# Two attention layers on one Trainium2 core: the second linear pass as an ordered pipeline, its end moved into the steps of the first row maxima

## The chip, the cores and the metric

The kernel runs on one core of one Trainium2 chip. The metric is the device time of one execution in microseconds (us); lower is better. The kernel before took 1602.39 us, the median of three runs (1594.55 to 1605.56). All engines of the core work on the same problem: PE multiplies matrices and transposes, DVE, ACT and POOL work on tiles in SBUF, and SP issues the DMAs. Each engine takes its instructions in the order of its own queue and waits at an instruction whose inputs or buffers are not ready. What stands behind a waiting instruction on that engine waits too. The trace's times are those of one profiled execution, counted from the start of its span.

## What is computed

The input x has 2048 rows of 512 numbers, in 32 heads of 16. Four layers add to it in turn, A, B, A, B:

```python
x = x + A(layernorm(x))     # A, per head:
#   pq, pk = q @ w_phi, k @ w_phi
#   phi(p) = [softmax(p), softmax(-p)]             32 features
#   o = phi_q (phi_k^T v) / (phi_q (sum of phi_k)); A = o @ wo
x = x + B(layernorm(x))     # B, per head, four segments of 512 rows, s = 0..3:
#   p = softmax(q k^T / 4 + causal mask) @ v       inside the segment
#   m = phi(q) M / (phi(q) z + 1e-6)               memory of the segments before
#   o = g m + (1 - g) p;  M += phi(k)^T v;  z += sum of phi(k);  B = o @ wo
```

All arithmetic is in float32. A projection is done as three products of a high and a low part (hi x hi, lo x hi, hi x lo), each of which PE takes at its fast rate.

## The kernel before

**Layer A in two passes.** The first pass (`pass1`, L564) goes over the four segments, the last one being segment 0 (`SEGS`). For a segment it normalises and transposes the rows (`norm_T`, L353), projects k, q and v, forms the features of k and adds phi_k^T v to an accumulator, whose end is the tile `KN`. For q it keeps the projected rows: those of segment 0 stay in SBUF as `P` tiles, those of the others go to memory (`pq`) with their row extremes (`mmq`). The second pass (`pass2`, L737) goes over the 16 tiles of 128 rows. For tile i: take the differences of pq and its extremes on POOL, the exponential on ACT, the reciprocals of the sums on DVE and their product on POOL (`feats`, L731, with `differences` L519, `scale_q` L544); transpose the features on PE in two halves, which ACT copies out of PSUM; multiply them by KN on PE; divide on DVE (`weigh`, L448: rows `tmp`); transpose the divided rows of the tile before (`turn`, L419: ACT makes `oh`, DVE makes `ol`); multiply by wo (`out_proj`, L438); and add the residual on DVE, which SP then writes. PSUM tiles of the name `g` come from three banks (`G`).

**Layer B as a table of steps.** `steps` (L1059) runs a counter k from -31 to 163. From k = -9 on a step computes products for row maxima (PE `mx`, DVE `mx` and `mxs`), from k = 0 on also logits and exponentials (PE `lg`, ACT `P`), and PE's product with v follows (`pv`). Everything else (projections of q, k and v, norms, memory, output, the first pass of the next layer A) is put into single steps by the tables `BEFORE`, `FIRST`, `GAPS`, `LAST`, `FINAL`. `opening` (L1048) comes ahead of `steps`: `start` (L785) lets SP fill parts of the four tiles of Q and K with the mask and ones, the first norm of layer B is taken to its 11th step (loads of x, statistics, normalisation), and the weights bwv and the first two slices of wqk are loaded (`queue_w`, L805).

**Who sets the order.** A scheduler orders the instructions of each queue by its own model, except where the program adds dependences: `Ordered` (L153) chains what is issued on DVE, ACT, POOL and SP while `ordered[0]` is set, and `held` (L173) chains PE's while `strict[0]` is set. Before the change, the second pass has neither. The main loop takes 63 yields of it (`A20`, L41), runs the whole opening, sets PE's order as strict, and gives the rest of the pass to `steps`, which spreads it over the slots k = -31 to 1 up to an amount of PE work (`LEFT`, L38). DVE, ACT, POOL and SP are ordered from k = -9 (`ORDERED`, L40). So SP could issue early what stands late in the program: it issued the slices of wqk at 174.68 us and bwv at 180.60, in the first pass, and the loads of the norm as soon as their rows had been written.

**The start.** In the first layer `pass1` loads ident, bd and z, two halves of the raw k weights, x, and the other raw weights. It normalises the first rows while the k weights are folded with w_phi (`folded`, L278), splits the weights (`bring`, L237), and projects v.

Of the kernel before, what the change touches and what calls it, by code (L numbers as in the profile page):

```python
# [7 lines left out]
F32 = mybir.dt.float32  # L8
# [7 lines left out]
D = 512  # L16
H = 32
DH = 16
# [87 lines left out]
def interleave_kernel(ctx, tc, x_in, a_wqkv, a_wphi, a_wo, b_wq, b_wk, b_wv, b_wo, b_beta,  # L106
# [88 lines left out]
    sync.dma_start(out=ident, in_=c_ident)  # L195
    bd = cp.tile([P, 25], F32, name="bd")
    sync.dma_start(out=bd, in_=c_bd)
# [80 lines left out]
    def folded(raw, banks=None):  # L278
# [8 lines left out]
        def get(kc, pf=None):  # L287
            if pf is None:
                pf = PS("g", G)
            for c in range(NC):  # L290
                mm(pf[:, c * P : (c + 1) * P], lhsT=wT[:, c, kc * P : (kc + 1) * P],
                                 rhs=phibd[:, c].rearrange("p h f -> p (h f)"), start=True, stop=True)
            return pf
        if banks is None:
            return get
        done = [get(kc, banks[kc // 2][:, kc % 2]) for kc in range(NC)]
        return lambda kc: done[kc]

    wph = T2("z16", 1, shape=(P, NC, DH))
    sync.dma_start(out=wph, in_=a_wphi.rearrange("(c h) d f -> (h d) c f", c=NC))  # L300
    phibd = sp.tile([P, NC, 8, DH], F32, tag="KN", bufs=1, name="phibd")
    for c in range(NC):
        pool.tensor_tensor(out=phibd[:, c], in0=wph[:, c, :].unsqueeze(1).broadcast_to([P, 8, DH]),
                                in1=bd[:, 16:24].unsqueeze(2).broadcast_to([P, 8, DH]), op=MUL)
# [48 lines left out]
    def norm_T(xsrc, s, hT, spare=False, slow=False, off=False):  # L353

        st = T2("st", 2, shape=(P, 4, 8))
        xt = []
        for t in range(4):
            x = T2("x", 4)
            sync.dma_start(out=x, in_=xsrc[4 * s + t])
            xt.append(x)  # L360
        yield
        for t, x in enumerate(xt):
            bs = T2("bs", 2, shape=(P, 6))
            dve.bn_stats(bs, x)
            dve.bn_aggr(st[:, t, 0:2], bs)
            if t < 3:
                yield
        var, r, u = st[:, :, 1], st[:, :, 2], st[:, :, 3]
        dve.tensor_scalar(var, var, 1e-5, None, op0=ADD)
        yield  # L370
        act.activation(u, var, AF.Ln)
        act.activation(r, u, AF.Exp, scale=-0.5)
        if slow:
            yield
        eng = pool if off else dve
# [5 lines left out]
        eng.tensor_scalar(u, u, -1.0, None, op0=MUL)  # L381
        if slow:
            yield
        for t in range(4):
            act.activation(xt[t], xt[t], AF.Identity, bias=st[:, t, 3:4], scale=st[:, t, 2:3])
# [3 lines left out]
        if spare:  # L389
            hh, hl = wtiles("e8")  # L390
        else:
            hh = hp_.tile([P, NC, D], F32R, tag="hh", bufs=1, name=nm("hh"))
            hl = hp_.tile([P, NC, D], F32R, tag="hl", bufs=1, name=nm("hl"))
        hT[:] = [hh, hl]
        for t in range(4):
            pt = PS("g", G)
            for kc in range(NC):
                tp(pt[:, kc * P : (kc + 1) * P], xt[t][:, kc * P : (kc + 1) * P], ident)
            pv = pt.rearrange("p (k t) -> p k t", k=NC)
            c0 = t * P  # L400
            hv = hh[:, :, c0 : c0 + P]
            act.copy(hv, pv)
# [825 lines left out]
```

## Time and profile before

| what | value |
|---|---|
| median of 3 runs | 1602.39 us (1594.55 to 1605.56) |
| profiled execution | 1599.14 us |
| its span, first to last instruction | 1597.4 us |
| mean granted clock of PE | 0.989 |
| busy share PE, DVE, ACT, POOL | 95%, 71%, 49%, 40% |
| first product with KN, layers 0 and 2 | 204.30 and 983.23 us |
| first product for maxima (k = -9), layer 1 | 316.66 us |
| first logits (k = 0), layer 1 | 348.05 us |
| first projection of v, layer 0 | 19.46 us |

A row of a timeline or of a group has the start, the time, the engine, the line, the operation, the tile written and the tiles read (without their numbers), shapes and the count; in brackets the idle time of the engine ahead of it, and what ended it. `PEld` is the load of weights into PE, which lies beside its products. A row of the waits names the engine that waited, what released it, the sum, the number of waits and the longest. A row of the windows gives the stretch and the busy time of each engine in it, then the granted clock as a share of full speed, the share of DMA time and GB/s. In the chain, each piece is what the next piece was waiting for. In the layers numbered from 0, A is 0 and 2, and B is 1 and 3; "the first pair" is layers 0 and 1.

### The profile page before, as it was taken

How to read it: one execution, taken by the hardware profiler on the slowest of the kernel's cores; microseconds unless marked ns; L12 is line 12 of the kernel's file. 1: busy time of each engine (PE TensorE's matmuls, PEld its weight loads, DVE VectorE, ACT ScalarE, POOL GpSimd, SP SyncE). 2: the span in 40 equal slices, each digit the busy share in tenths (PEclk: the TensorE clock that was granted, in tenths of full speed). 3: DMA queues.
4: the chain of work that ended last, by engine and by line, in shares of the span. 5: the costliest groups of instructions: out<-in, count | busy, mean ns of one | idle time of the engine just before them, and what ended most of it. 6: DMA issues, size and time to landing. Idle time of an engine off the chain costs nothing.

```text
span 1597.4 us, 28178 instructions
## 1 busy us (share of the span) xinstructions
PE 1512.8 (95%) x9856; PEld 1080.8 (68%) x9856; DVE 1127.4 (71%) x3286; ACT 789.6 (49%) x1180; POOL 638.9 (40%) x970
## 2 busy tenths in 40 slices
PE   7999999988999999999989999999889999999997
PEld 6888877855566666665568888877556666666554
DVE  5665776477788887878555648656787788787783
ACT  6544335335665565555433323443465655655543
POOL 1566643313444454333231337431234444443322
PEclk9999999999999999999999999999999999999999
DMA  8446543234433533534322125342353443433330
GB/s 319 132 142 221 204 137 122 100 103 150 127 106 100 153 94 100 153 94 138 103 105 77 36 95 168 122 145 87 111 171 97 109 137 101 107 115 99 81 105 36
DMA packets 101124, 195.76 MB, mean 123 GB/s; under 512 B 13560, under 2 KB 27128, under 8 KB 97912
## 3 DMA queue, kind: packets, MB, share of 16 engines
q1 hardware_dynamic: 99832, 193.44, 39.2%
q8 instruction: 79, 1.29, 0.3%
q10 hardware_dynamic: 1152, 0.52, 0.1%
q14 instruction: 61, 0.50, 0.1%
HBM read 101.05 MB, written 39.85 MB: 88 GB/s over the span
## 4 chain that ended last, share of the span: by engine, by line
PE 67%; DVE 16%; DMA 5%; ACT 4%; issue 4%; POOL 3%; SPq 1%; DVEq 0%; POOLq 0%; ACTq 0%
PE g L185 39%; DVE mx L163 9%; PE mx L185 9%; PE lg L185 8%; PE pv L185 7%; PE g L189 5%; POOL P L163 3%; DVE mxs L163 2%; DMA x<-x 1%; ACT P L163 1%; ACT tb L163 1%; DVE es L163 1%; SPq L163 1%; DVE bs L163 1%; DVE ta L163 1%
## 5 line engine op out<-in xcount | busy, mean ns | idle before, releaser
L163 DVE CUSTOM_DVE_ANT_0 mx<-mx,mask 128x128 f32<-128x128 f32 (+3 forms) x1024 | 510.9, 499 | 172.4 <-PE mx L185 137.4
L163 ACT ACTIVATE P<-lg 128x1024 f32<-128x1024 f32 x320 | 328.7, 1027 | 181.3 <-PE lg L185 172.3
L163 POOL TENSOR_SCALAR_AFFINE_SELECT P<-P 128x256 f32<-128x256 f32 (+1 forms) x448 | 190.1, 439 | 469.2 <-ACT P L163 467.9
L185 PE MATMUL mx<-e,e 63*128 63x256 f32 (+2 forms) x1024 | 155.7, 360 | 29.7 <-DVE mxs L163 21.9
L185 PE MATMUL g<-hh,wqk 128*128 128x512 f32 x512 | 180.7, 407 | 0.7 <-ACT mt L163 0.7
L185 PE MATMUL g<-w,oh 128*128 128x512 f32 x512 | 173.4, 421 | 4.0 <-ACT oh L163 2.7
L185 PE MATMUL lg<-e,e 64*128 64x256 f32 (+2 forms) x1024 | 168.3, 386 | 7.7 <-ACT P L163 5.6
L185 PE MATMUL g<-w,hh 128*128 128x512 f32 x512 | 168.3, 408 | 2.5 <-ACT tb L163 1.4
L185 PE MATMUL pv<-P,v 128*32 128x512 f32 (+3 forms) x2048 | 166.3, 441 | 0.0
L185 PEld LDWEIGHTS lg<-e,e 64*128 64x128 f32 x1024 | 81.1, 184 | 102.8 <-issue 54.2
L163 DVE DVE_READ_ACCUMULATOR2_ANT mxs<- 128x1 f32 x1024 | 144.7, 141 | 0.0
L185 PEld LDWEIGHTS mx<-e,e 63*128 63x128 f32 x1024 | 83.0, 185 | 80.0 <-DVE mxs L163 55.4
L185 PEld LDWEIGHTS pv<-P,v 128*32 128x32 f32 x2048 | 53.8, 109 | 99.2 <-issue 88.7
L163 POOL TENSOR_SCALAR tb<-tb 128x512 f32<-128x512 f32 x48 | 71.4, 1488 | 102.5 <-ACT tb L163 102.5
L185 PEld LDWEIGHTS g<-w,oh 128*128 128x128 f32 x512 | 91.8, 195 | 28.6 <-issue 6.0
L185 PEld LDWEIGHTS g<-hh,wqk 128*128 128x128 f32 x512 | 96.3, 188 | 21.8 <-ACT mt L163 1.2
L185 PEld LDWEIGHTS g<-w,hh 128*128 128x128 f32 x512 | 91.9, 190 | 24.0 <-ACT tb L163 3.5
L163 ACT CAST ta<-g 128x512 fp32r<-128x512 f32 x64 | 37.5, 586 | 135.7 <-PE g L185 135.7
L185 PE MATMUL g<-w,ol 128*128 128x512 f32 x256 | 102.5, 402 | 1.1 <-DVE ol L163 1.1
L185 PE MATMUL g<-w,hl 128*128 128x512 f32 x256 | 101.4, 396 | 0.0
L185 PE MATMUL g<-hl,wqk 128*128 128x512 f32 x256 | 100.2, 391 | 0.0
L185 PE MATMUL g<-w,e 128*128 128x512 f32 x384 | 98.2, 397 | 0.8 <-ACT tb L163 0.8
(122 smaller groups left out, 2601.9 us busy)
## 6 DMA issues: line engine op xcount, KB each, us to landing
e<-ta SPq DMA_DIRECT2D x384, 128.0 KB
wqk<-wqk SPq DMA_DIRECT2D x64, 512.0 KB
x<-x SPq DMA_DIRECT2D x48, 256.0 KB
xr<-in SPq DMA_DIRECT2D x28, 256.0 KB
pq<-tb SPq DMA_DIRECT2D x24, 256.0 KB
tb<-pq SPq DMA_DIRECT2D x24, 256.0 KB
x<-xr SPq DMA_DIRECT2D x24, 256.0 KB
xr<-x SPq DMA_DIRECT2D x24, 256.0 KB
```

The source lines that it names most:

```text
L163: i = f(*a, **k)
L185: return held(nc.tensor.matmul(*a, **k))
L189: return held(nc.tensor.transpose(*a))
```

## The change

1. The second pass is written as a pipeline and kept in written order on all engines, PE too. With tile i, POOL takes the differences of tile i+3, ACT the exponential of i+2, DVE and POOL the scaling of i+1, and SP loads pq of i+4. The rows of the first three tiles come over from the first pass as raw differences.
2. The main loop takes 76 yields of it: all of tiles 0 to 8 but the output of tile 8. `opening` yields after each of its 11 steps of the norm. It is advanced at k = 42, 45, ..., 75: the fills and the loads of x come in tile 5, bwv and two slices of wqk behind the output of tile 7. Then come the 16 transposes of the norm and the projections of `BEFORE`. DVE, ACT, POOL and SP are in written order there too.
3. The rest of the pass (output of tile 8, tiles 9 to 15) goes into the slots k = -9 to 1 alone, in place of -31 to 1 (`LEFT` 44000).
4. The start is a function of its own, `first`, in written order: x is loaded ahead of ident, bd, z and the raw weights; the statistics of all four tiles are one chain; two of the four tiles are normalised on DVE; some low parts go to POOL; q is folded behind the first half of v's projection. Layer A's wq lies in the buffers `e8`, and in the second layer A a spare normalised segment in `w8`. `PREP` goes from 12 to 6, and the first segment of the first pass is strict, with the order k0 k1 q0 q1 v0 k2 k3 q2 q3 v1.
5. At the end of layer B the following work is taken in four single steps around the last turn, and PE's strict order holds to the end.

The number of instructions is the same on PE (8096 in the program), DVE (3286) and SP (795). Two normalisations move from ACT (1243 to 1241) to DVE, and two low parts from DVE to POOL (970 to 972). The core of the diff, with the new function `first` in it:

```diff
@@ -34,15 +34,14 @@
 FILL = (1, 3, 4)
 LEAD = 9
 FINAT = 8
-PAUSE = object()
-LEFT = 53000
+PAUSE, DONE = object(), object()
+LEFT = 44000
 BEGIN = -31
-ORDERED = -9
-A20 = 63
-PREP = 12
+MAXIMA = -9
+A20 = 76
+PREP = 6
 EVERY = (2, 2)
 SEGS = (1, 2, 3, 0)
-AHEAD = 2
 TB2 = 4
 
 
...
+        def first(self, hT, vv):
+
+            ordered[0] = strict[0] = True
+            xt = rows_of(self.xsrc, SEGS[0])
+            wph = T2("z16", 1, shape=(P, NC, DH))
+            sync.dma_start(out=ident, in_=c_ident)
+            sync.dma_start(out=bd, in_=c_bd)
+            sync.dma_start(out=wph, in_=a_wphi.rearrange("(c h) d f -> (h d) c f", c=NC))
+            kraw, vraw, qraw = [fetch(a_wqkv[:, i * D : (i + 1) * D]) for i in (1, 2, 0)]
+            st = T2("st", 2, shape=(P, 4, 8))
+            hT[:] = htiles()
+            (vh, vl), (kh, kl), (qh, ql) = wv, wk, wq = [wtiles(tag) for tag in ("w8", "w8", "e8")]
+            for key, w in (("awv", wv), ("awk", wk), ("awq", wq)):
+                kept[key] = [dtile((P, NC, D), nm(key)) for _ in range(2)]
+                owed.extend(zip(kept[key], w))
+
+            def low(eng, w, kc, raw):
+                eng.tensor_tensor(out=w[1][:, kc, :], in0=raw, in1=w[0][:, kc, :].bitcast(F32), op=SUB)
+
+            for t in range(4):
+                moments(st, t, xt[t])
+            guard(st)
+            root(st)
+            refine(st, dve)
+            for c in range(NC):
+                pool.tensor_tensor(out=phibd[:, c], in0=wph[:, c, :].unsqueeze(1).broadcast_to([P, 8, DH]),
+                                        in1=bd[:, 16:24].unsqueeze(2).broadcast_to([P, 8, DH]), op=MUL)
+            kf, qf = [], []
+            kfold, qfold = folded(kraw, kf), folded(qraw, qf)
+            normal(st, 0, xt[0])
+            for t in (1, 3):
+                dve.tensor_scalar(xt[t], xt[t], st[:, t, 2:3], st[:, t, 3:4], op0=MUL, op1=ADD)
+            next(kfold)
+            next(kfold)
+            normal(st, 2, xt[2])
+            columns(hT, 0, xt[0])
+            columns(hT, 1, xt[1])
+            next(kfold)
+            next(kfold)
+            columns(hT, 2, xt[2])
+            columns(hT, 3, xt[3])
+            next(kfold)
+            for kc in range(NC):
+                act.copy(vh[:, kc, :], vraw[kc])
+                low(pool if kc % 2 else dve, wv, kc, vraw[kc])
+            for kc in range(NC):
+                act.copy(kh[:, kc, :], kf[kc])
+                low(dve, wk, kc, kf[kc])
+            vt = v_tile(hT, wv, vv, ("g", G))
+            for t in range(4):
+                for _ in range(4):
+                    next(vt)
+                if t == 1:
+                    for _ in range(4):
+                        next(qfold)
+            next(qfold)
+            for kc in range(NC):
+                act.copy(qh[:, kc, :], qf[kc])
+                low(dve, wq, kc, qf[kc])
+            ordered[0] = strict[0] = False
+            floor.update(ends)
+            return wq, wk, wv
...
@@ -668,11 +711,15 @@
 
                 if n < NSEG - 1:
                     hTs, vv = [], []
-                    side = chain(norm_T(self.xsrc, SEGS[n + 1], hTs, n % 2 == 0), v_tile(hTs, wv, vv, ("g", G)))
+                    spare = ("e8" if first else "w8") if n % 2 == 0 else None
+                    side = chain(norm_T(self.xsrc, SEGS[n + 1], hTs, spare), v_tile(hTs, wv, vv, ("g", G)))
                     steps = "k0 q0 k1 q1 v0 k2 q2 k3 q3 v1"
+                    strict[0] = first and n == 0
+                    if strict[0]:
+                        steps = "k0 k1 q0 q1 v0 k2 k3 q2 q3 v1"
...
@@ -721,31 +759,23 @@
                         dve.tensor_tensor(out=KN, in0=kva.rearrange("p g (h e) -> p g h e", e=VW),
                                           in1=bdA[:, 0:4].unsqueeze(1).unsqueeze(3).broadcast_to([P, 8, 4, VW]),
                                           op=MUL)
-                        floor.update({k.engine: ends[k.engine] for k in (dve, sync)})
-                        ordered[0] = False
-                strict[0] = False
-                scale(5)
-                self.put_off[4 * s + 2] = lambda: scale_q(e.pop(6))
+                self.e = {4 * s + t: e[4 + t] for t in range(3)}
                 yield
 
-        def feats(self, i):
-
-            pq = T2("tb3", 2)
-            sync.dma_start(out=pq, in_=self.pqs[i])
-            return scale_q(diff_exp(pq, self.mmq[i // 8][:, i % 8]))
+        def load_q(self, i):
+            if i < NT:
+                pq = T2("tb3", 2)
+                sync.dma_start(out=pq, in_=self.pqs[i])
+                self.raw[i] = pq, self.mmq[i // 8][:, i % 8]
 
         def pass2(self):
 
+
             KN = self.KN
             o = None
             for i in range(NT + 1):
                 if i < NT:
-                    j = i + AHEAD
-                    if j in self.put_off:
-                        self.e[j] = self.put_off.pop(j)()
-                    elif j < NT and j not in self.e:
-                        self.e[j] = self.feats(j)
-                    ef = self.e.pop(i)
+                    ef = self.e.pop(i).rearrange("p h s f -> p (h s f)")
                     phT = T2("P4", NP4, shape=(P, 8, P))
                     for half in range(2):
                         pt = PS("g", G)
@@ -753,11 +783,15 @@
                             g = 4 * half + q
                             tp(pt[:, q * P : (q + 1) * P], ef[:, g * P : (g + 1) * P], ident)
                         act.copy(phT[:, 4 * half : 4 * half + 4, :], pt.rearrange("p (g t) -> p g t", g=4))
+                        if half == 1 and i + 1 < NT:
+                            scale_q(self.e[i + 1])
                         yield
                 if i > 0:
                     oT = turn([o[:, c * P : (c + 1) * P] for c in range(NC)])
-                    yield
+                    yield PAUSE if i == NT else None
                 if i < NT:
+                    if i + 2 < NT:
+                        exp(self.e[i + 2])
                     o = T2("tmp", 2)
                     for half in range(2):
                         pn = PS("g", G)
@@ -769,6 +803,9 @@
                         weigh(o[:, half * 256 : half * 256 + 256].rearrange("p (g h d) -> p g h d", g=4, h=4),
                               pv, 0.0, False)
                         yield
+                    if i + 3 < NT:
+                        self.e[i + 3] = differences(*self.raw.pop(i + 3))
+                    self.load_q(i + 4)
                 if i > 0:
                     yield from out_proj(x, self.xdst, i - 1, oT, self.wo)
                 if i < NT:
...
@@ -1052,6 +1091,7 @@
             self.norm0 = self.norm(0)
             for _ in range(11):
                 next(self.norm0)
+                yield
             self.wv = load_w("bwv")
             for _ in range(2):
                 self.queue_w()
@@ -1130,11 +1170,11 @@
                         at_, *what = cell.split()
                         m, j = at_.split(".")
                         table[8 * R * s + R * int(m) + int(j)] = what, s
-            slots = list(range(BEGIN, 2))
+            slots = list(range(MAXIMA, 2))
             spent = 0.0
             for k in range(BEGIN, R * N + 4):
                 m = k // R + 3
-                ordered[0] = ORDERED <= k < R * N
+                ordered[0] = k < R * N
                 if k % R == 0 and 0 <= m < N:
                     self.stack(m)
                 if 0 <= k < R * N:
@@ -1155,22 +1195,29 @@
                     want = LEFT * (1 + slots.index(k)) / len(slots) if k < slots[-1] else 1e9
                     while spent + 100 < want:
                         before = work[0]
-                        if next(side, None) is PAUSE:
-                            break
+                        got = next(side, DONE)
                         spent += work[0] - before
+                        if got is DONE or got is PAUSE and k < slots[-1]:
+                            break
                 what, s = table.get(k, ((), 0))
                 for w in what:
                     do(w, s, k)
                 if k == R * N - 1:
-                    strict[0] = ordered[0] = False
+                    ordered[0] = False
                     floor.update(ends)
             put_off[0] = None
             for f in self.late + self.rows:
                 f()
+            next(after, None)
             self.finish(N - 1)
             for _ in early:
                 pass
-            self.end()
+            for _ in range(2):
+                next(after, None)
+            o = self.end_turn()
+            next(after, None)
+            self.end(o)
+            strict[0] = False
 
     class DTiles:
         def __init__(self, full):
@@ -1190,11 +1237,14 @@
         lb = LayerB(xs[2 * i + 1], xs[2 * i + 2])
         run(p1[i])
         a2 = la[i].pass2()
-        for _ in range(A20):
+        opening = lb.opening()
+        for k in range(A20):
             next(a2)
-        lb.opening()
-        strict[0] = True
-        lb.steps(chain(a2, iter(lambda: PAUSE, 0)), p1[1] if i == 0 else iter(()), FINAL if i else LAST)
+            if k >= 42 and k % 3 == 0:
+                next(opening, None)
+        for _ in opening:
+            pass
+        lb.steps(a2, p1[1] if i == 0 else iter(()), FINAL if i else LAST)
 
 
 def kernel(A_x, A_wqkv, A_w_phi, A_wo, B_x, B_wq, B_wk, B_wv, B_wo, B_beta):
```

More of the change, by code (lines that the diff above doesn't have):

```diff
@@ L276, in plain, with folded @@
         return get
-    def folded(raw, banks=None):
+    def folded(raw, chunks):
         wT = T2("e8", 2 * NSET, shape=(P, NC, D))
@@ L388, in norm_T @@
         yield
[L389 to L394, printed above, removed]
-        for t in range(4):
[L396 to L402, printed above, removed]
-            wait(lambda pv=pv, hv=hv, c0=c0: dve.tensor_tensor(out=hl[:, :, c0 : c0 + P], in0=pv,
-                                                               in1=hv.bitcast(F32), op=SUB))
+        hT[:] = htiles(spare)
+        for t in range(4):
+            columns(hT, t, xt[t])
             yield
@@ L593, in pass1 @@
+                wq, wk, wv = self.first(hTs, vv)
             else:
+                norm = norm_T(self.xsrc, SEGS[0], hTs, slow=True, off=True)
                 for _ in range(11):
@@ L597, in pass1 @@
                 wv = load_w("awv")
-            for _ in norm:
-                yield
-            vt = v_tile(hTs, wv, vv, ("g", G))
-            if first:
-                next(vt)
-                wq = load_w("awq", folded(qraw), "e8")
-            if not first:
+                for _ in norm:
+                    yield
+                vt = v_tile(hTs, wv, vv, ("g", G))
                 for _ in range(8):
```

161 lines of the change are left out of this document (72 added, 89 removed).

## The prediction

> **What bounds the kernel now.** I read the page first, for the engine that fills the span and for the chain that ended last.
>
> ```profile
> span 1597.4 us, 28178 instructions
> PE 1512.8 (95%) x9856; PEld 1080.8 (68%) x9856; DVE 1127.4 (71%) x3286; ACT 789.6 (49%) x1180; POOL 638.9 (40%) x970
> PE 67%; DVE 16%; DMA 5%; ACT 4%; issue 4%; POOL 3%; SPq 1%; DVEq 0%; POOLq 0%; ACTq 0%
> ```
>
> PE is busy for 1512.8 of 1597.4 us, so all its idle time together is 84.6 us. The change gives every engine the same work as before and only moves it. It can therefore win idle time back, or lower-clock time, and nothing else; what it can lose has no such limit. The profiled execution took 1599.14 us, 1.74 above its span and 3.25 below the median of the three runs (1602.39).
>
> Next come the windows over the part that is rewritten, first in the first pair of layers: from the first product with KN to the third step of attention (step 2). The second pair's same part follows. The columns are the window, its length, busy time of PE, PEld, DVE, ACT and POOL, and the granted clock.
>
> ```profile
> 204.30:265.00 60.70, 54.32 (x350) 46.91 (x351) 43.00 (x99) 27.19 (x43) 31.50 (x36) 0.97 0.41 131
> 265.00:316.66 51.66, 50.42 (x291) 42.83 (x290) 23.53 (x51) 20.32 (x34) 16.08 (x20) 1.00 0.35 113
> 316.66:348.05 31.39, 25.55 (x144) 18.06 (x143) 23.14 (x76) 6.92 (x13) 2.75 (x2) 1.00 0.32 101
> 348.05:353.43 5.38, 5.38 (x29) 3.48 (x28) 3.71 (x13) 2.81 (x4) 0.81 (x2) 1.00 0.82 197
> 983.23:1135.17 151.94, 138.74 (x810) 114.20 (x810) 93.69 (x239) 57.25 (x94) 51.18 (x59) 0.97 0.41 129
> ```
>
> The four rows make 149.13 us with PE busy for 135.67: 13.46 idle, 6.38 in the first row and 5.84 in the third, where the first row maxima stand. The clock of 0.97 over 60.70 us is 1.7 us of full-clock time lost, so the stretch holds some 134.0 us of work. The second pair needs 151.94, 2.8 more, all of it in PE's busy time (138.74), that is, in clock. The waits name what the idle time is.
>
> ```profile
> PE g L189 <- DVE ot L163: 2.0, 2, 1.6
> PE g L185 <- ACT P L163: 1.6, 3, 1.1
> PE g L189 <- POOL P L163: 1.5, 1, 1.5
> PE g L189 <- DVE hl L163: 1.0, 1, 1.0
> PE mx L185 <- DVE mxs L163: 2.7, 3, 1.0
> ```
>
> Many short waits, on every engine: there is no single one to take away. (Four rows are from before the maxima, the last from the maxima.)
>
> **The change, part by part.** *The pipeline itself.* PE's rows of one tile of the second pass:
>
> ```profile
> 227.61 1.03 PE L189 MATMUL g<-ident,P 128*128 128x128 f32 x8
> 228.62 0.66 PE L189 MATMUL g<-ident,tmp 128*128 128x128 f32 x4
> 229.11 1.90 PE L185 MATMUL g<-KN,P 128*128 128x68 f32 x16
> 230.82 0.71 PE L185 MATMUL g<-w,oh 128*128 128x512 f32 x2
> 233.66 1.04 PE L189 MATMUL g<-ident,P 128*128 128x128 f32 x8
> ```
>
> One tile is 6.05 us (227.61 to 233.66): 1.01 for the transposes of phi_q, 0.49 for those of the divided product, 1.71 for KN, 2.84 for the output projection. It runs without a gap already. In written order the first pass's last reductions stay ahead of tile 1's on DVE, so the wait on POOL's P (1.5) becomes some 1.8; four following tiles cost about 0.3. Taken: 2.1 idle; bounds 0 to 4.
>
> *The norm's loads on SP.* The opening (mask and ones into the sets, the loads and statistics of layer B's first norm) now starts at k = 42, in tile 5, and SP takes it in written order: the write of x row 3, six fills, then the four loads. SP's rows:
>
> ```profile
> 174.68 1.00 SPq L163 DMA_DIRECT2D wqk<-wqk  x2
> 180.60 0.80 SPq L163 DMA_DIRECT2D w<-bwv  x2
> 202.79 0.70 SPq L163 DMA_DIRECT2D e<-mask  x1
> 204.20 2.50 SPq L163 DMA_DIRECT2D e<-mask  x3
> 208.92 0.63 SPq L163 DMA_DIRECT2D e<-ones  x1
> 211.30 0.56 SPq L163 DMA_DIRECT2D e<-ones  x1
> 217.86 0.39 SPq L163 DMA_DIRECT2D x<-x  x1
> 256.56 2.63 DMA x<-x
> ```
>
> The fills cost SP 0.70 + 2.50 + 0.63 + 0.56 = 4.39 us. They come behind the write that follows the add of tile 3, so with that write and the next residual load (about 1 us) the first norm load is issued some 6 us after the add, and lands 2.63 later (the last row, from the chain): 8.5. On DVE the statistics of that row stand behind tile 5's division, about 3.5 us after the same add by the tile's prices (1.01 + 0.49 + 1.71 and the division's end). Behind them on DVE wait the add of tile 4, which holds its PSUM bank, then the reduction of tile 7, then `ol` of tile 5, for which PE's next projection waits. DVE is 5.0 us late there, a tile has 6.05 us and DVE some 4.8 of work (43.00 in the first window over nine tiles), so about 1.1 is made up and PE loses about 3.9. Bounds 0 (the write is done early) and 5.
>
> *bwv and the first two slices of wqk.* Before, SP issued them at 174.68 and 180.60, with the rest of pass 1 as cover. Now they stand behind the write of x row 7. That write waits for the add of tile 7, which waits for the end of its projection. After that projection PE has only the 16 transposes of the norm. By rows: add 0.69, write 0.6, so the loads start 1.3 us after the projection. A slice of wqk is 512 KB and stands behind 2 MB of bwv: 2.62 MB. The rate and the time to land are in these rows (the first two are the rates in 40 slices of 0.7 us and the hardware queue's sum from 172 to 200 us, with packets, MB and share; the others a load of weights and PE's wait for it):
>
> ```profile
> GB/s 433 398 360 398 407 401 421 378 389 427 345 331 357 401 404 474 354 404 375 410 410 386 222 82 35 0 0 0 0 0 0 0 0 23 0 0 0 0 0 0
> q1 hardware_dynamic: 1983, 6.28, 58.0%
> 826.79 8.87 DMA w<-awq_lo
> 835.71 0.50 PE L185 MATMUL g<-w,hh 128*128 128x512 f32 x1 [1.15 <-DMA w<-awq_lo]
> ```
>
> The transfers fill 23 slices, 16.1 us: 6.28 MB in that time is 390 GB/s, so 2.62 MB take 6.7, and with 1.8 of latency (2.63 less 256 KB at that rate) 8.5: 9.8 after the projection. PE reaches the first q group after 2.0 of transposes and 1.6 of their waits, at 3.6. It waits 6.2 us. Bounds: 3 (wqk overtakes bwv: 0.52 MB need 1.4 + 1.8, and v needs its weights one group later) and 8.9 (the row of awq). Nothing hides it, since PE's order is written out there and nothing else stands before q. The Trainium skill ("DMA: Bandwidth & Descriptors", Specifications) puts a core's limit on its memory at about 358 GB/s; by that the same bytes would take 7.3 and the wait would be an estimated 6.8. The measured 390 lies above the limit, so the trace decides and 6.2 stands.
>
> *16 transposes in a row.* Three PSUM banks for four groups: the fourth waits for ACT's copy and DVE's `hl`. Before, this was the 1.0 on `hl` and part of `ot`; now 1.5 in one place. Bounds 1 and 2.5.
>
> *The maxima.* Tiles 9 to 15 and the end of 8 lie in steps -9 to 1 alone. At step -9 ACT has in front of tile 9's copies what these rows show:
>
> ```profile
> 316.77 0.58 ACT L163 CAST ta<-g 128x512 fp32r<-128x512 f32 x1 [4.62 <-PE g L185]
> 319.91 1.09 ACT L163 ACTIVATE tb<-g 128x512 f32<-128x512 f32 x2 [2.56 <-DVE ta L163]
> 320.88 0.81 ACT L163 ACTIVATE x<-x,st 128x512 f32<-128x512 f32 x1
> 321.58 1.07 ACT L163 COPY P<-g 128x512 f32<-128x512 f32 x2
> ```
>
> The `tb` wait for DVE's `ta`, which is written behind four first maxima. The first copy of a tile ends at 321.58 + 0.53 = 322.11, 5.45 after step -9 began (316.66). PE has 0.49 of maxima, 1.01 of transposes and 0.49 more as cover, 2.0, so 3.5 idle, with handover 3.6. Later steps: PE has about 45.3 us of work there and DVE about 45.8, nearly balanced; taken 2.1 for steps -8 to -1 and 1.9 for steps 0 and 1, where `ol` of tile 15 stands behind maxima. Bounds of the later steps together: 0 and 11.
>
> *Clock.* The rows of the boundary show what idle time costs afterwards:
>
> ```profile
> 815.01 0.66 PE L189 MATMUL g<-ident,U 128*128 128x128 f32 x4 [0.81 <-ACT U L163]
> 819.49 0.66 PE L189 MATMUL g<-ident,tmp 128*128 128x128 f32 x4 [1.75 <-POOL tmp L163]
> 820.82 2.07 PE L185 MATMUL g<-w,oh 128*128 128x512 f32 x4 [0.68 <-ACT oh L163]
> ```
>
> Four matmuls took 2.07 after 1.75 + 0.68 us of idle; two take 0.71 at 230.82. Over the slow stretch that is some 1.7 us. I take two such stretches for each pair, 3.4 us: after the wait of 3.9 or the one of 3.6, and after that of 6.2. The Trainium skill ("TensorE: Matmul & The Clock Gate", What's actually happening) has the clock halve after an idle window of about 3.4 us. By that rule only the 6.2 is sure of it, and the sum would be 1.7 less for each pair. The trace shows a slow stretch after 2.4 us of idle in two pieces, so two are kept.
>
> *The sum for a pair.* 134.0 of work + 2.1 + 3.9 + 1.5 + 6.2 + 3.6 + 2.1 + 1.9 idle + 3.4 clock = 158.7. Against 149.13 that is +9.6, against 151.94 +6.8: together +16.4.
>
> *The start.* Normalisation and folding are rewritten; the first projection of v starts here:
>
> ```profile
> 3.23 1.99 SPq L163 DMA_DIRECT2D x<-in  x4
> 18.70 1.11 PE L189 MATMUL g<-ident,x 128*128 128x128 f32 x4 [1.24 <-DVE hl L163]
> 19.46 1.20 PE L185 MATMUL g<-w,hh 128*128 128x512 f32 x2
> ```
>
> x is now issued first, 2.4 us sooner, but PE's chain also needs ident and the raw weights, which come 2 us later. By my hand count v starts at 18.9 to 19.1: -0.4 us (bounds -3 and +2).
>
> *Boundary and end.* A group of k covers the wait for U (0.81), and wq goes into other buffers, which spares the 1.15 on awq_lo: with the shorter gaps -2.2 (0 to -4.5). Two steps of the following work interleave with the last turn; in the last layer, where nothing follows, the strict order to the end costs 0.3. Earlier preparation and the strict first segment of pass 1 lie beside dense PE work, at nothing (if PE waits there, up to 2).
>
> Sum: 16.4 - 0.4 - 2.2 + 0.3 = +14.1. 1599.1 + 14.1 = 1613.2, taken as 1613.
>
> **Rivals.** *The loads are in time.* If the norm rows are there when DVE wants them and the first slice lands within 3.6 us of the end of tile 7's projection (2.3 after issue), the waits of 3.9 and 6.2 go, and one slow stretch with them: 158.7 - 11.8 = 146.9, that is -2.2 and -5.0, and with the rest 1599.1 - 7.2 - 2.3 = 1589.6. For it speaks that 256 KB alone land in 2.63; against it, that 2 MB go first on the same queue. The point where the change breaks even is a loss of 7.05 less for each pair: both waits together 3.1 instead of 10.1.
>
> *One of the two is hidden.* Only the weights late: 1613 - 7.8 = 1605; only the norm rows late, with a slow stretch less: 1613 - 15.8 = 1597.
>
> *DVE bounds the maxima.* Balanced sums do not mean that the chain copy, KN, division, turn, `ol` fits between maxima: the idle share in the third row is 5.84 of 31.39, 19%. If the eleven steps with 45.3 us of work keep that share, idle time there is 10.6 instead of 7.6, +6 over both; if every one of seven tiles loses 1 us more besides, +20: 1619 to 1633, taken 1626. It decides when DVE ends each step behind PE by more than a PSUM bank covers.
>
> **How the numbers follow.** Late loads in both places, as summed: 0.50, 1604 to 1622. In time: 0.22, 1579 to 1596 (down to where no slow stretch is left either, 3.4 less). One hidden: 0.14. DVE in the maxima: 0.14. The range for 8 in 10, 1588 to 1628, reaches into both rivals and leaves out the lower third of the one and the upper third of the other, with the tails. About 1% is what a measurement of this kernel can tell from no change (its own runs spread over 0.7%); from 1602.39 that puts the bounds at 1586 and 1618. Slower: the DVE case and two fifths of the first, 0.34. Faster: the lower half of the loads in time with its tail, 0.11. Within: 0.55. My likeliest case is within 1%, on the slow side.
>
> **What would show it.** Right: PE idle for 5 to 8 us in front of the first matmul of `g<-hh,wqk` in each pair, released by the DMA of wqk or bwv, with half-speed rows behind it; DVE's first statistics of the norm released by the DMA of x some 4 us late, in tile 5; ACT's copies of P at step -9 behind `tb`. Wrong: q follows the transposes at once; the tiles take 6.1 us through tile 5; the maxima take much more or less than 51 us for steps -9 to -1. A forecast too high by 10 or more means that the loads were not late, and one too low by 10 that DVE sets the pace in the maxima.

## The result, and the profile after

The changed kernel takes 1653.03 us, the median of 6 runs (1650.82 to 1656.99), against 1603.12 for the kernel before in 6 runs. The ratio is 1.0319 with a 95% interval of 1.0287 to 1.0351: 3.2% slower. The forecast was 1613, with a range to 1628. The page of the profile after, its first lines, and PE's own waits (engine, line, what it waited for, the sum, how many, the longest):

```profile
span 1655.3 us, 28153 instructions
PE 1532.1 (93%) x9856; PEld 1094.4 (66%) x9856; DVE 1135.8 (69%) x3286; ACT 786.9 (48%) x1178; POOL 643.3 (39%) x972
```

```profile
PE g L184 <- DVE xr L162: 18.5, 2, 9.7
PE g L184 <- DMA wqk<-wqk: 15.9, 2, 8.1
PE mx L184 <- DVE mxs L162: 15.6, 31, 1.5
...
PE g L188 <- ACT x L162: 8.1, 1, 8.1
PE g L184 <- DVE ol L162: 6.8, 6, 1.7
...
PE mx L184 <- DVE r L162: 4.4, 8, 0.8
```

The span is 57.9 longer. Some 8 of that is the choice of executions: the one profiled before lies 4 under its median (1603.12), the one after 4 over. PE's idle time went from 84.6 to 123.2 (+38.6), and its busy time, for the same products, from 1512.8 to 1532.1 (+19.3). Two waits stand out that were not there before, or only in pieces of up to 1.2: on `xr` and on wqk, twice each, once in each pair. (`xr` and `ot` are tiles with the residual; DVE's add into them frees the PSUM bank that PE writes next. `hh` and `hl` are the high and low parts of the normalised, transposed rows.) By stage:

| from, to | before | after | difference |
|---|---|---|---|
| start to first projection of v | 19.46 | 19.13 | -0.3 |
| to the first product with KN, layer 0 | 184.84 | 193.08 | +8.2 |
| to step 3's logits, layer 1 | 150.80 | 176.24 | +25.4 |
| to the first product with KN, layer 2 | 628.13 | 629.76 | +1.6 |
| to step 3's logits, layer 3 | 153.61 | 175.60 | +22.0 |
| to the end | 460.56 | 461.49 | +0.9 |

So the loss lies in the two rewritten stretches and in the first 60 us. The windows of the first pair after (length, busy PE, PEld, DVE, ACT, POOL, then the granted clock):

```profile
212.21:259.87 47.66, 36.81 (x237) 32.48 (x237) 25.57 (x57) 16.80 (x26) 18.59 (x18) 0.90 0.37 110
259.87:290.80 30.93, 21.38 (x116) 17.93 (x117) 17.42 (x38) 10.54 (x18) 10.85 (x17) 0.78 0.56 196
290.80:314.50 23.70, 23.70 (x97) 19.22 (x98) 5.75 (x12) 6.46 (x13) 4.04 (x8) 0.92 0.58 174
314.50:388.45 73.95, 65.70 (x367) 51.20 (x366) 49.90 (x139) 24.44 (x40) 18.06 (x18) 0.91 0.36 106
```

They add up to 176.24 us with PE busy for 147.58: 28.66 idle. The same stretch before had 136.46 busy and 14.34 idle. The clock is under 1.00 in all four rows; before it was under 1.00 in the first alone. The rows of the timeline behind these windows, PE first, then SP and DVE:

```profile
259.87 1.98 PE L184 MATMUL g<-KN,P 128*128 128x68 f32 x8 [8.79 <-DVE xr L162]
263.00 1.22 PE L184 MATMUL g<-w,oh 128*128 128x512 f32 x2 [1.16 <-DVE ol L162]
290.80 0.77 PE L184 MATMUL g<-hh,wqk 128*128 128x512 f32 x1 [8.06 <-DMA wqk<-wqk]
318.88 1.11 PE L188 MATMUL g<-ident,tmp 128*128 128x128 f32 x4 [2.80 <-ACT tb L162]
320.06 3.68 PE L184 MATMUL g<-KN,P 128*128 128x68 f32 x16
```

```profile
242.92 0.32 SPq L162 DMA_DIRECT2D x<-xr  x1
243.28 0.44 SPq L162 DMA_DIRECT2D xr<-in  x1
244.12 1.38 SPq L162 DMA_DIRECT2D e<-mask  x2
249.35 0.63 SPq L162 DMA_DIRECT2D e<-ones  x1
250.08 1.31 SPq L162 DMA_DIRECT2D e<-mask  x2
254.98 0.55 SPq L162 DMA_DIRECT2D e<-ones  x1
255.58 1.82 SPq L162 DMA_DIRECT2D x<-x  x4
```

```profile
258.31 0.69 DVE L162 BATCH_NORM_STATS2 bs<-x 128x6 f32<-128x512 f32 x1 [11.84 <-DMA x<-x]
```

SP issues two fills of the mask by 245.5 and then nothing until 249.35; two more by 251.4, and then nothing until 254.98. Each gap ends in a fill of ones, and SP's own waits (two such gaps in each pair) put them down to the landing of the mask:

```profile
SPq L162 <- DMA e<-mask: 15.7, 4, 4.9
```

The loads of x come 12.7 us after the write of x row 3 (242.92), and DVE stands for 11.84 us in front of the first statistics.

### The profile page after: what moved, and what is told of

Same layout as the page of the kernel before. It is cut to its first block, busy times and chain, and to the rows that moved or that the text cites. A ratio compares the mean times of both kernels' runs of the same rounds, so it can differ in the third digit from the quotient of the medians.

```text
span 1655.3 us, 28153 instructions
## 1 busy us (share of the span) xinstructions
PE 1532.1 (93%) x9856; PEld 1094.4 (66%) x9856; DVE 1135.8 (69%) x3286; ACT 786.9 (48%) x1178; POOL 643.3 (39%) x972
## 4 chain that ended last, share of the span: by engine, by line
PE 71%; DVE 16%; issue 4%; ACT 4%; DMA 3%; POOL 2%; SPq 1%; ACTq 0%; DVEq 0%; POOLq 0%
PE g L184 43%; DVE mx L162 8%; PE mx L184 8%; PE lg L184 8%; PE pv L184 6%; PE g L188 6%; DVE mxs L162 2%; POOL P L162 1%; ACT tb L162 1%; ACT P L162 1%; DMA wqk<-wqk 1%; DVE es L162 1%; DVE ta L162 1%; DVE bs L162 1%; SPq L162 1%
## 5 line engine op out<-in xcount | busy, mean ns | idle before, releaser
L184 PE MATMUL g<-w,oh 128*128 128x512 f32 x512 | 177.4, 429 | 9.1 <-DVE ol L162 5.7
L184 PE MATMUL g<-w,hh 128*128 128x512 f32 x448 | 146.6, 408 | 3.5 <-ACT tb L162 3.0
L184 PEld LDWEIGHTS g<-w,hh 128*128 128x128 f32 x448 | 80.6, 190 | 23.1 <-ACT tb L162 5.1
L162 POOL TENSOR_TENSOR P<-P,rr 128x512 f32<-128x512 f32 x32 | 33.9, 1060 | 151.2 <-DVE rr L162 151.2
L162 ACT COPY P<-g 128x512 f32<-128x512 f32 x64 | 34.7, 589 | 116.5 <-PE g L188 116.5
```

What stands on the lines that cost most here:

```text
L162: i = f(*a, **k)
L184: return held(nc.tensor.matmul(*a, **k))
```

## The experiments

Each kernel was run beside the kernel before, and the ratio is to that; the medians of before were 1600.7 to 1602.3, and 1603.1 beside the changed kernel. Differences to the changed kernel carry these 2.4 us too.

### The weights ahead of the second pass

`weights` holds the loads of bwv and of the first two slices of wqk, taken out of `opening`.

```diff
+        lb.weights()
         opening = lb.opening()
```

> One part is undone: bwv and the first two slices of wqk are issued ahead of the second pass, not behind its tile 7. Theory 1 (each wait costs its own length and a slow-clock stretch behind it): PE's waits on the DMA of wqk (8.06 and 7.87, 15.9 together) go, and with them some 1.9 us of half clock in each pair (granted clock 0.92 over the 23.7 us behind the wait): 1653 - 19.7 = 1633 us, PE's busy sum falls from 1532.1 to about 1528. Theory 2 (the lower clock belongs to the new order itself): only the waits go, 1637, PE busy stays at 1532. Theory 3 (the wait moves: 3 MB ahead of the tiles' loads make pq or the residual late): idle falls by less than 8, 1645 or more, and the new wait stands on tb or xr in tiles 0 to 4.

Measured: 1634.97 us, ratio 1.0219 (1.0183 to 1.0255), 18 less than the changed kernel. The wait on wqk is gone (in its place 0.68 on `hh` and 0.22 on `hl`), the wait on `xr` stays, and PE is busy for 1527.5, 4.6 less. The time alone does not tell theory 1 (1633) from theory 2 (1637). The first row with wqk does: it took 0.77 in the changed kernel, and now runs at full speed:

```profile
284.15 0.50 PE L184 MATMUL g<-hh,wqk 128*128 128x512 f32 x1 [0.68 <-ACT hh L162]
```

From it to the first maxima it is 22.5 us, where the changed kernel takes 23.7, and the granted clock is 0.974 to 0.976 in the four runs, against 0.967 to 0.972 in the six of the changed kernel. That is theory 1: the wait and its clock, nothing late in its place.

### The loads of x ahead of the fills

```diff
-            self.start()
             self.norm0 = self.norm(0)
-            for _ in range(11):
+            next(self.norm0)
+            self.start()
+            yield
+            for _ in range(10):
```

> Another part is changed: the four loads of x of layer B's first norm stand ahead of the fills of mask and ones on SP, in the same step. Theory 1: DVE gets the first row in time, so the waits on xr (8.79 and 9.71) and on ol behind them (1.16 and 1.17) go, 20.8, and the half clock behind them (0.78 over the 30.9 us from 259.87, some 4.4 us lost in each pair): 1653 - 29.6 = 1623, PE busy about 1523. Theory 2: waits alone, 1632, PE busy 1532. Theory 3: the fills, now behind, hold SP twice for the landing of the mask and make the loads of pq or the writes of x late: 1640 or more, with POOL's differences waiting for the DMA of tb.

Measured: 1647.86, ratio 1.0291 (1.0246 to 1.0336): 5 less where 30 was expected, and the two intervals overlap. The timeline of this run, DVE, SP and POOL:

```profile
262.35 0.69 DVE L162 TENSOR_TENSOR ot<-g,ot 128x512 f32<-128x512 f32 x1 [9.33 <-DMA ot<-in]
```

```profile
243.41 1.97 SPq L162 DMA_DIRECT2D e<-mask  x2
250.43 0.63 SPq L162 DMA_DIRECT2D e<-ones  x1
251.17 1.32 SPq L162 DMA_DIRECT2D e<-mask  x2
256.17 0.55 SPq L162 DMA_DIRECT2D e<-ones  x1
256.82 0.34 SPq L162 DMA_DIRECT2D tb<-pq  x1
```

```profile
259.81 1.06 POOL L162 TENSOR_TENSOR P<-tb,mmq 128x512 f32<-128x512 f32 x1 [9.25 <-DMA tb<-pq]
```

x was in time, but SP stood still in the same two places, and now DVE stood 9.3 in front of the residual of a later tile and POOL 9.3 in front of pq; PE waited 7.3 on `ot`. Theory 3 holds. What is short is not a load but SP's queue.

### Both together

The two diffs above.

> Both changes together: the weights ahead of the second pass, and x ahead of the fills. Theory 1: the two effects add, 1653 - 19.7 - 29.6 = 1604, as fast as the kernel before; PE busy about 1519. Theory 2: 1653 - 36.7 = 1616 with PE busy at 1532. Theory 3: what one takes away is waited for elsewhere, over 1625.

Measured: 1626.85, ratio 1.0174 (1.0132 to 1.0216), PE busy 1528.6. It is 21 less than x_first alone, so the weights' part adds as it should; the fills' part still does not.

### Why SP stands still: ones behind all masks

```diff
                 for t in (Q, K):
                     dma(t[3:P:4].rearrange("p a t -> p (a t)"),
                         mask[0:32, 0:P].unsqueeze(1).broadcast_to([32, 16, P]))
-                dma(K[63:P:64].rearrange("p a t -> p (a t)"), ones[0:2, :].unsqueeze(1).broadcast_to([2, 16, P]))
+            for Q, K in self.sets:
+                dma(K[63:P:64].rearrange("p a t -> p (a t)"), ones[0:2, :].unsqueeze(1).broadcast_to([2, 16, P]))
```

> On the changed kernel only the order of the six fills is changed: the four of the mask first, then the two of ones. It tells what holds SP there. Theory A (each fill of ones waits for the landing of the mask under it, 4.2 to 6.3 us in the traces, and SP's queue waits with it): one of the two waits falls away, so the loads of the norm are issued some 4 to 5 us sooner (255.6 to about 251), the waits on xr fall from 8.8 and 9.7 to about 4.5 each: 1653 - 9 and some clock = 1641 to 1645. Theory B (the issue of the fills, 4.4 us, is the cost, as in the forecast): nothing changes, 1653.

Measured: 1644.84, in two executions only, ratio 1.0261 (1.0213 to 1.031). Both are faster than all six of the changed kernel. PE's waits on `xr` fell from 18.5, and SP's for the mask from 15.7, to

```profile
PE g L184 <- DVE xr L162: 12.6, 2, 7.2
SPq L162 <- DMA e<-mask: 7.2, 4, 2.6
```

The order alone of six fills took 8 us off the median; 5.9 of it stand in the waits on `xr`, 1.6 in the first pair and 4.3 in the second. Row 63 of K is among the rows that the mask writes (3, 7, ..., 63, ...), so the fill of ones must find the mask's landed; it waits for that at the head of SP's queue. This is theory A, but less of it than expected (the waits on `xr` are 7.2 and 5.4, not 4.5): the fills of ones still wait, now for four masks in a row, of which the last took 6.36 to land in the first pair.

### The fills ahead of the pass, the weights behind x

```diff
+        lb.start()
         opening = lb.opening()
```

`start` holds the six fills. In the opening, behind its first step, stand bwv and two slices of wqk.

> Both loads set right: the fills ahead of the second pass, the loads of x in the opening's first step as before, bwv and the first slices of wqk in its second. Theory A (the landing waits of the fills hold SP for some 12 us, and whatever is behind them is late: x in the changed kernel, the residual and pq with x ahead): ahead of the pass SP has room, so the waits on xr, ot and wqk go in both pairs, 36.7 us, with some 13 of clock: about 1603. If only the waits go and the clock stays: 1616. Theory C (the next load is late instead, pq of tiles 4 and 5 behind the fills): over 1620, with POOL waiting for the DMA of tb.

Measured: 1627.55, ratio 1.0154 (1.0122 to 1.0185): 25 less than the changed kernel, not 50. PE's idle time fell by 23.4 and its busy time by 4.0, where 36.7 and some 13 were expected. Two pieces of this run's chain show why not all the waits went (start, length, what):

```profile
222.74 2.85 DMA xr<-in
...
251.78 11.10 DMA ot<-in
```

The first is a residual that SP could issue at 222.74 only, behind the fills. The second is a residual of 256 KB that took 11.1 us to land, with 3 MB of weights issued ahead of it at 248.21. PE waited 3.62 for it, and 1.79 for the first; POOL waited 5.71 for pq at 225.09, the sign of theory C. So theory C holds here: with x, residual and pq needed in each tile, 3 MB in the middle of the pass make the next of them late. Why so little of the clock came back, no run takes apart.

### The statistics of the second segment ahead of q's fold

PE not strict in the first segment (`unstrict`):

```diff
-                    strict[0] = first and n == 0
-                    if strict[0]:
+                    if first and n == 0:
```

> One part is undone: PE's order is not strict in the first segment of the first pass; the order string stays. Theory 1: PE can project on while the norm of the next segment waits for DVE, so the waits in the first 60 us (8.10 on x, 1.91 and 0.63 on e) go, and some 1.7 us of clock behind them: 1653 - 12 = 1641, and the first product with KN comes at about 200 instead of 212.2. Rival: the norm's statistics stay behind q's low parts on DVE, so the same wait comes at the next place where PE needs the transposed rows: 1650, KN at 209 or later.

Measured: 1652.45, ratio 1.0322 (1.0282 to 1.0362), as slow as the changed kernel. The wait of 8.10 on x is gone from PE, and this stands in its place:

```profile
46.53 0.70 PE L184 MATMUL lg<-v,P 128*128 128x68 f32 x2 [6.08 <-POOL P L162]
```

The rival holds: strictness on PE is not the cause. In the changed kernel DVE sits still until q's fold has passed through PE and ACT, and the statistics of the next segment are written behind it:

```profile
34.70 0.69 DVE L162 TENSOR_TENSOR e<-lg,e 128x512 fp32r<-128x512 f32 x1 [11.16 <-ACT e L162]
...
38.59 1.28 DVE L162 BATCH_NORM_STATS2 bs<-x 128x6 f32<-128x512 f32 x2
```

So the next kernel writes them ahead of it (`fills_stats`, on top of fills_early):

```diff
+            self.n1 = norm_T(self.xsrc, SEGS[1], self.h1, "e8")
+            for _ in range(6):
+                next(self.n1)
             vt = v_tile(hT, wv, vv, ("g", G))
```

> As fills_early, and in the start the statistics and the normalisation of the second segment are written ahead of q's fold, so that DVE does not reach them behind q's low parts, which wait for PE until 34 us. If that order on DVE is the cause of the wait of 8.10 (and of 6.08 on P with PE not strict): 10.6 of waits and about 1.5 of clock less than fills_early, about 1591, and the first product with KN at some 200. If the strict order itself is the cause: the same wait elsewhere, within 3 us of fills_early.

Measured: 1629.74, ratio 1.0166 (1.013 to 1.0203), no better than fills_early. Now ACT has the normalisation in front of the copies of v:

```profile
32.59 2.82 PE L188 MATMUL g<-ident,P 128*128 128x128 f32 x12 [6.77 <-ACT v L162]
```

The wait went from DVE's order into ACT's. The time alone would also fit the strict order as the cause; `unstrict` speaks against that, and `best`, below, settles it. The version below puts the statistics ahead on DVE and the normalisation behind the copies on ACT.

### The rest of the pass from step -12

```diff
-MAXIMA = -9
+MAXIMA = -12
```

> As fills_early, and the rest of the second pass begins at step -12 in place of -9, with the same amount of work over 14 slots in place of 11. If ACT's order at step -9 (copies of tile 9 behind tb, which wait for ta behind four maxima) is what the maxima's first step costs: the wait of 2.80 and about 4.5 us of half clock behind it go in each pair, and of the later 1.70 on ol and its clock a part: 12 to 18 less than fills_early, about 1588. If DVE bounds the whole stretch: the wait moves to later steps, within 4 us of fills_early.

Measured: 1618.04, ratio 1.0093 (1.0058 to 1.0129), 9.5 less than fills_early, where 12 to 18 were expected. The wait of 2.80 on `tb` is gone in both pairs, but PE waits for `ta` in its place, 4.3 in all.

### A version without the waits, and its parts

`spread_m12` has the weights ahead of the pass, x in the opening's first step, and the six fills one for each later step, masks first, one step without a fill, then ones; the rest from step -12 on.

> bwv and the first slices of wqk ahead of the second pass; the loads of x in the opening's first step; the six fills one for each later step, all masks first and ones last, so that no fill meets a landing it must wait for on SP; the rest of the pass from step -12 on. Theory A (the loss in tiles 1 to 6 is SP's queue waiting for landings, or a load standing behind 3 MB of weights; nothing else): the waits on ot (7.6), xr (4.2) and their clock (about 3) that fills_m12 still had go: 1618 - 15 = 1603. Theory C (some load is always late, since a tile has three of them): over 1612.

Measured: 1600.44, ratio 0.9993 (0.9974 to 1.0012). Theory A: the mask is no longer among SP's waits, the waits on wqk are gone, those on `xr` and `ot` come to 0.9 and 1.2, and 53 us of the changed kernel's time are back. Some 10 of them belong to the start at step -12 (`fills_m12`).

`best` adds the start's two orders (five steps of the norm ahead of v's projection, the sixth behind the copies for q's fold):

> As spread_m12, and in the start the statistics of the second segment ahead of q's fold on DVE, its normalisation on ACT behind the copies of q's weights, which fills_stats had ahead of the copies of v (wait of 6.8 on v in place of 8.1 on x). If the two orders on DVE and ACT are the cause of the waits in the first 60 us: 8.10 + 1.9 + 0.6 and about 1.5 of clock go, 12 less than spread_m12, about 1591, under the kernel before (1600.7). If the strict order is the cause: within 4 of spread_m12.

Measured: 1593.36, ratio 0.994 (0.9918 to 0.9962). It is 0.6% faster than the kernel before, the fastest of all, and 7 less than spread_m12, where 12 were expected. The first product with KN comes at 201.83, against 211.43 in spread_m12. Before it was 204.30; the two kernels below, with the same start as best, have it at 204.32 and 206.02, so the new start is not shown to be faster than the old one. Up to 60 us PE has no wait of over 1 us but the one for the first weights.

`best_m9` is best with the rest from step -9 again, `best_m20` from step -20.

> As best, but the rest of the second pass starts at step -9 again, as the change has it. This prices that one choice with the other waits gone. If ACT's order at step -9 costs it (wait of 2.80 on tb, 0.52 on the copies, some 4.5 us at half clock behind them, 1.70 on ol with 1.7 of clock at step -6, less the 2.35 that best waits at its own first tile): 8 to 9 in each pair, so 14 to 18 above best, about 1609, with the wait on tb in the profile again. If best's gain over spread_m12 is all that matters and the start step does not: within 4 of best, 1590 to 1597.

> As best, with the rest of the second pass from step -20 on (22 slots): tiles 9 and on begin among the projections of steps -20 to -10. If the maxima steps are short of cover for the tiles' chains (copy, KN, division, turn), more of the tiles lie beside dense projections: 3 to 8 less than best. If at -12 the chains are covered: within 3; if DVE or ACT is short in the projections too: 3 or more above.

Measured: best_m9 1606.79, ratio 1.0028 (1.0006 to 1.005); best_m20 1601.63, ratio 1.0005 (0.9985 to 1.0024). So step -12 is better than both: by 13 and by 8. PE's rows at the first tile of the first pair, best_m9 first, then best (which waits 2.22 there in the second pair):

```profile
293.43 1.11 PE L188 MATMUL g<-ident,tmp 128*128 128x128 f32 x4 [2.81 <-ACT tb L162]
```

```profile
279.64 0.66 PE L188 MATMUL g<-ident,tmp 128*128 128x128 f32 x4 [1.16 <-DVE ta L162]
```

And PE's waits in the maxima, best first, then best_m20:

```profile
PE mx L184 <- DVE mxs L162: 15.9, 32, 1.5
PE mx L184 <- DVE r L162: 4.4, 8, 0.8
```

```profile
PE mx L184 <- DVE mxs L162: 20.1, 36, 1.5
PE mx L184 <- DVE r L162: 6.6, 10, 1.1
```

From -9 the first tile has too little cover; from -20 too much of the rest is gone when the maxima come, and they wait for DVE, 6.4 us more in all. These waits are the largest difference in the lists; the rest of the 8 was not taken apart. The kernel before, which began at -31, has 28.5 of these two waits, 8.2 more than best:

```profile
PE mx L185 <- DVE mxs L163: 21.9, 40, 1.5
PE mx L185 <- DVE r L163: 6.6, 10, 1.1
```

## Why the prediction was wrong, point by point

The direction and the two main waits were right; the size was not, and one step was wrong altogether. For the first pair (us; the measured clock is PE's 147.58 less 134.7 of work at full clock, the forecast's 134.0 with step 2 to 3 added):

| step of the forecast | forecast | measured |
|---|---|---|
| tile 1 and the tiles after it | 2.1 | 2.05 |
| the norm's loads on SP (`xr`, then `ol`) | 3.9 | 9.95 |
| 16 transposes | 1.5 | 0.34 |
| bwv and the slices of wqk | 6.2 | 8.06 |
| step -9 | 3.6 | 2.80 |
| later steps | 4.0 | 4.3 |
| lower clock | 3.4 | 12.9 |

Against the profiled execution the sum was 43.8 too low: 31.0 in the two stretches up to step 2, 8.3 ahead of the first product with KN, 3.9 at the boundary, 0.7 at the end. Two slips in the working are small: 2.63 less 256 KB at 390 GB/s leaves 1.96 of latency, not 1.8, and 6.05 less 4.8 is 1.25, not 1.1.

- **The norm's loads.** The forecast priced the six fills at the 4.39 us that SP takes to issue them. The runs show that the two of ones also wait for the mask under them to land, up to 4.9 us each, with SP's queue behind them: 12.7 from the write to the loads of x, in place of 6. The rows quoted in the forecast held a sign of it: SP was done with the masks at 206.70 (204.20 + 2.50), and its first fill of ones came at 208.92. SP waited for the mask before the change too, 10.5 us in four waits, but at the start of the pass, where the rows that the norm loads were not written yet (its first load came at 217.86). `ones_last` and `x_first` tell it apart from issue time. This was a wrong mechanism inside a right step.
- **The weights.** The mechanism was right, and the price mis-sized by 1.9. PE came to the first q group 2.65 after the projection, not 3.6 (the transposes waited 0.34), and the slice landed 10.6 after it instead of 9.8. `w_early` showed that all of it comes back.
- **The clock.** This is the largest term that was mis-sized, 9.5 in the first pair. The forecast had two stretches of 1.7 us each. The changed kernel has the clock below 1.00 after nearly every wait of over a microsecond, and for longer than that price allows: the window from 320 to 328 us is at half speed throughout, behind a wait of 2.80:

```profile
320.00:328.00 8.00, 7.94 (x26) 6.35 (x27) 2.85 (x8) 1.94 (x4) 4.32 (x4) 0.50 0.12 35
```

  With the waits gone, best is busy for 1505.9 us in its profiled execution, 26.2 less than the changed kernel, and its six runs have a granted clock of 0.988 to 0.995, against 0.967 to 0.972: the clock follows the waits. In single steps it did so loosely (x_first and fills_early lost idle time and kept PE busy within 4 us).
- **The start.** The first projection of v was forecast 0.4 sooner and came 0.33 sooner. The rest of `first` and of the first segment was put at nothing, or up to 2. It cost 10.6 us in three waits before 60 us (+8.2 on the stage). This step failed outright: the forecast followed PE's order and did not follow DVE's, where the statistics of the second segment are queued behind q's low parts, 11.16 us idle. `best` against spread_m12 shows that it is a matter of two orders, on DVE and ACT.
- **The boundary** was forecast at -2.2; the stage is +1.6. U's wait is 0.29, twice, in place of 0.81, and the one on awq_lo is gone, as forecast, but POOL's `tmp` costs 2.50 (1.75 before), and PE is busy 3.2 longer. No run takes this apart; it stays open how much of it is clock alone.
- **Step -9** was right in its place and its cause (`tb` behind `ta`), and near in size: 2.80 for 3.6. With the clock behind it and the later `ol` it is worth 13 us by best_m9 against best: 11.1 in the first pair's stretch and 2.7 in the second's, in the two profiled executions.
- **The rivals.** That DVE bounds the maxima did not happen: the waits on mxs and r are 20.0 in sum after, 28.5 before. So a forecast too low by 10 or more did not mean, as it said, that DVE sets the pace: steps -9 to -1 took 59.35 in place of 51, and PE was busy for 53.28 of them, at a granted clock of 0.88. The rest of the pass does cover waits in the maxima, but a gain in time is not shown there: the stretch from the first product with KN to step 3 takes 150.06 in spread_m12 and 147.36 in best, with the same code, against 150.80 before. The range ended 25 us too low since its upper end was built from that rival alone and not from the clock and the start.

## What to carry to other kernels

When a queue is put in written order, price a DMA on it not by its issue but by what it waits for: one fill that must see another land stops every load behind it, and moving one load ahead only chooses another to be late. Follow each engine's written order, not only the busiest one's, across the seams of the change: here DVE, ACT and SP held PE, in that turn. And price a wait of PE with the slow stretch behind it, which here lasted up to 9.6 us, and not with its length alone.

## What the runs showed of the hardware that was not expected

- Half speed lasted some 9.6 us after a wait of 2.8 us (318.88 to 328.50 in the changed kernel, where KN's 16 products took 3.68 in place of 1.90), while in step 3 of layer 1 a wait of 0.95 was followed by a slow stretch at 390 us after the change, and one of 0.88 by none at 355 us before it. The Trainium skill ("TensorE: Matmul & The Clock Gate", What's actually happening) has the clock fall after an idle window of about 3.4 us; this trace shows it fall after waits shorter than that (2.80, and 1.76 at 215.98).
- 256 KB that land in 2.6 to 2.9 us alone took 11.10 in `fills_early`, behind 3 MB issued 3.6 us ahead of them on the same queue.
- The fills of the mask within SBUF, 256 KB each, took 4.1 to 7.4 us to land (4.12 in `x_first`, 4.18 in the changed kernel, 7.42 in `both_early`).
